# Convolution in bursts of two quads, and what its PSUM bank does between them: attention beside a long convolution on one core

## The chip, the core and the metric

One Trainium2 chip, one of its cores. A core has a matrix engine (TensorE, PE in the profile), a vector engine (VectorE, DVE), an engine for functions such as the exponential (ScalarE, ACT), GpSimd (POOL) and SyncE (SP); the last two issue most of the transfers here, which 16 DMA engines carry. Matrix products land in PSUM, eight banks of 128 partitions x 512 fp32 values; everything else lies in SBUF. The engines run side by side, each through its own list of instructions in order, and wait for each other by semaphores. The metric is the device time of one execution in microseconds (us).

## What is computed

Two independent blocks, joined along the last axis. A is attention: 2048 positions, 512 features, 32 heads of 16. B is a gated long convolution (H3): `kv` is a four-tap filter of `k` times `v`, convolved with a filter of 2048 taps per channel (`ssm_k`, with `ssm_D` added for the direct path), times `q`.

```python
def _A_ref(x, wqkv, wo):
    q, k, v = qkv[0], qkv[1], qkv[2]          # of x @ wqkv, per head
    scores = jnp.einsum("bhqd,bhkd->bhqk", q, k) * (Dh ** -0.5)
    p = _softmax(scores, axis=-1)
    o = jnp.einsum("bhqk,bhkd->bhqd", p, v)
    return o.transpose(0, 2, 1, 3).reshape(B, S, D) @ wo

def _B_ref(q, k, v, shift_k, ssm_k, ssm_D):
    ...
    kv = k_shift * v
    ...
    y = y + kv * ssm_D[None, None, :]         # y: kv convolved with ssm_k along S
    return q * y
```

The exponential of the scores is the large part of A: 32 heads x 2048 x 2048 = 134 million values.

## The kernel before

**A program written by a planner.** Python code (lines 540 to 1225) walks through the work chunk by chunk and appends instructions to one list per engine, in the order in which each engine will run them. Class `Eng` keeps a planned clock for each engine (`pe.t`, `dve.t`) and for each handle the planned time at which it will be done (`at(...)`); `dma` does the same for transfers, one after the other, at `DMA_KB` a microsecond and no sooner than `late` us after their issue. The planner decides by these times what comes next; on the chip the semaphores alone hold.

**Scores.** The work of A is 32 groups (four output column blocks `o` x four blocks of 512 queries x two), each of 64 blocks: a block is 128 keys x 512 queries of one head, and fills one PSUM bank. There are 2048 of them. `emit_qk(T)` takes the next chunk: `take_banks(T)` says which banks are free, even chunks from bank 0 up, odd ones from bank 5 down, up to `MOST` = 3 each. TensorE writes the scores (`qk_mm`, line 675, 32 rows a head, so that blocks of different heads run side by side), and ScalarE takes the exponential of the whole chunk in one instruction over its neighbouring banks (`emit_exp`, line 708), into the ring `PT` of 18 blocks. While ScalarE works on one chunk, TensorE fills the other banks.

**VectorE's blocks.** Some blocks go to VectorE instead (`dve_block`, `exp_on_dve`): line 750 reads the bank into `FX`, then three polynomial steps (line 757) and a last one (762) that leaves the block in `PTD`. The last block of a chunk of at least three is chosen, and its bank is `hold`-ed: ScalarE's chunk is then two blocks. `PV`, the product with the values (`emit_pv`, line 791), follows two chunks later into bank `PVB` = 6.

**Units.** Projections (`q`, `k`, `v`), the products that make `kv`, output products (`op`) and the transposes of finished convolution output (`turn`) are units of one bank each. Up to chunk `N_OPEN` = 68 they run in bank `BGB` = 7. Afterwards a *window* gives them a bank: when a unit falls due within `OPEN` = 80 chunks, `take_banks` holds one score bank for `LEN` = 3 chunks or more (`win`), and `unit_step` puts the units in, each as two halves, followed by an evacuation by VectorE. Chunks beside a window have a bank less. `jobs` lists the due chunks, from a planned total of `PLAN` = 710.

**Convolution.** From chunk 68 on, bank `BGB` belongs to the convolution. Channels go in quads of four, 128 quads. A quad needs its filters as shifted rows, `WR`: four loads of 512 KB by SP from the DRAM tensor `kz_scratch` (`load_wr`); `WR` has room for four quads, and the next load is issued when a quad's last product is done. A quad is 16 *lags*, each of four small products side by side (`conv_lags`, line 961). Four quads fill a bank; then VectorE copies it to `YB` (line 975, 512 columns). After eight quads a `turn` transposes `YB` (line 986), and line 995 multiplies by `q`. `emit_bg` says how many lags a chunk gets: at most `LAGS` = 6, no more than a running budget (`lags`, fed so that the convolution ends by `PLAN` - `END`, times `PACE`), and no more than fits before ScalarE would have to wait (`room`, with `MARGIN` = 0.35 us to spare). A quad starts when its load is planned to have landed `WAIT` = 1.5 us ago.

**Filler.** `warm_up` (line 1166) puts products with zero weights into TensorE's gaps, onto a bank in which a sum is open.

## Time and profile before

| | us |
|---|---|
| median of three runs | 841.38 (840.96 to 846.39) |
| span of the profiled execution | 840.8 |
| first exponential starts, last one ends | 9.67, 833.67 |
| TensorE clock granted, mean | 0.999 |
| filters read: 512 loads of 512 KB | 268 MB |
| data moved, mean over the span | 347 GB/s |

How to read the profile: its engine line gives busy time, share of the span and number of instructions. A group line reads "line engine operation out<-in shapes xcount | busy us, mean ns of one | idle time of the engine ahead of them, and who ended it". Busy time counts overlapping instructions once, while the mean is of each one's own duration. A line of waits reads "engine line <- releaser: us in total, times, longest". A line of windows gives start and end of a stretch, the busy time of each engine in it with the number of instructions, then the granted clock, the DMA share and GB/s.

Other groups that the text speaks of, from the same page:

```profile
L675 PE MATMUL PS<-QT,KTo 32*128 32x512 bf16 x2048 | 286.6, 384 | 34.6 <-ACT PT L708 6.6
L791 PE MATMUL PS<-PT,VA 128*32 128x512 bf16 x1820 | 196.8, 389 | 2.0 <-DVE DT L852 0.6
L1166 PE MATMUL PS<-IDN,ZW 128*32 128x512 bf16 (+4 forms) x632 | 162.4, 335 | 0.2
L757 DVE SCALAR_TENSOR_TENSOR EH<-EH,FX 128x512 f32<-128x512 f32 x456 | 305.1, 687 | 0.0
```

### The profile page before, as it was taken

To read this page: it belongs to the slowest core of one execution; us is meant where nothing else is said; L and a number is where in the kernel's file an instruction comes from. 1 tells how busy PE (TensorE), PEld (TensorE's weight loads), DVE (VectorE), ACT (ScalarE), POOL (GpSimd) and SP (SyncE) were. 2 spreads that over 40 slices of the span, in tenths; PEclk is the share of its full clock that TensorE was granted. 3 is DMA by queue.
4 is the path that set the end of the run, shared out by engine and by line. 5 is a ranking of instruction groups with operands and counts; after the bars stand their busy time and mean duration, and the time that the engine had idled before them with its cause. 6 is when DMAs were issued, how large, how long until landed. Compare 5 with 4: busy or idle time off the path is not lost.

```text
span 840.8 us, 30758 instructions
## 1 busy us (share of the span) xinstructions
PE 792.8 (94%) x13774; PEld 333.3 (40%) x13774; DVE 814.7 (97%) x1392; ACT 825.8 (98%) x726; POOL 77.6 (9%) x155
## 2 busy tenths in 40 slices
PE   8999999999999999999999999999999999999997
PEld 3343334444343434344434334443433333333442
DVE  3999999999999999999999999999999999999996
ACT  6999999999999999999999999999999999999997
POOL 3200220010100101000110010101002020000000
PEclk9999999999999999999999999999999999999999
DMA  9997199999999999999999999999999999999952
GB/s 230 216 310 285 50 371 370 354 347 408 392 408 394 393 402 338 371 326 378 330 379 408 384 340 359 377 405 398 406 408 379 351 394 409 409 316 391 405 200 76
DMA packets 109235, 291.42 MB, mean 347 GB/s; under 512 B 37680, under 2 KB 41648, under 8 KB 108720
## 3 DMA queue, kind: packets, MB, share of 16 engines
q1 hardware_dynamic: 102256, 280.80, 90.6%
q0 software_dynamic: 5648, 8.27, 3.2%
q8 instruction: 109, 1.79, 0.9%
q10 hardware_dynamic: 1200, 0.39, 0.2%
q14 instruction: 22, 0.18, 0.1%
HBM read 276.83 MB, written 6.42 MB: 337 GB/s over the span
## 4 chain that ended last, share of the span: by engine, by line
ACT 92%; PE 3%; DVE 3%; DMA 1%; issue 0%
ACT PT L708 92%; DVE EH L757 2%; PE PS L675 1%; PE PS L791 1%; DMA xT<-in_A_x_dram 1%; PE PS L961 1%; DVE PTD L762 1%; DVE FX L750 1%; PE PS L536 0%; PE PS L415 0%; PE PS L1166 0%; DVE DT L852 0%; ACT QT L920 0%; DVE DTN L863 0%; PE PS L902 0%
## 5 line engine op out<-in xcount | busy, mean ns | idle before, releaser
L708 ACT ACTIVATE PT<-PS 128x1536 bf16<-128x1536 f32 (+2 forms) x721 | 822.9, 1455 | 2.6 <-PE PS L675 2.6
L675 PE MATMUL PS<-QT,KTo 32*128 32x512 bf16 x2048 | 286.6, 384 | 34.6 <-ACT PT L708 6.6
L757 DVE SCALAR_TENSOR_TENSOR EH<-EH,FX 128x512 f32<-128x512 f32 x456 | 305.1, 687 | 0.0
L961 PE MATMUL PS<-WR,KV 128*15 128x128 bf16 (+15 forms) x8192 | 213.4, 219 | 1.1 <-issue 1.1
L791 PE MATMUL PS<-PT,VA 128*32 128x512 bf16 x1820 | 196.8, 389 | 2.0 <-DVE DT L852 0.6
L961 PEld LDWEIGHTS PS<-WR,KV 128*1 128x1 bf16 (+15 forms) x8192 | 144.7, 87 | 82.3 <-issue 47.1
L675 PEld LDWEIGHTS PS<-QT,KTo 32*128 32x128 bf16 x2048 | 72.7, 91 | 234.4 <-ACT PT L708 185.3
L1166 PE MATMUL PS<-IDN,ZW 128*32 128x512 bf16 (+4 forms) x632 | 162.4, 335 | 0.2
L750 DVE TENSOR_SCALAR FX<-PS 128x512 f32<-128x512 f32 x228 | 156.9, 690 | 2.4 <-PE PS L675 1.3
L762 DVE SCALAR_TENSOR_TENSOR PTD<-EH,FX 128x512 uint16<-128x512 f32 x228 | 155.7, 685 | 0.0
L757 DVE SCALAR_TENSOR_TENSOR EH<-FX 128x512 f32<-128x512 uint16 x228 | 155.7, 689 | 0.0
L259 POOL DMA_DIRECT2D QT<-QS x120 | 58.7, 497 | 481.5 <-DVE QS L442 165.7
L791 PEld LDWEIGHTS PS<-PT,VA 128*32 128x32 bf16 x1820 | 47.5, 93 | 108.6 <-issue 97.7
L791 PE MATMUL PS<-PTD,VA 128*32 128x512 bf16 x228 | 68.3, 383 | 0.3 <-DVE PTD L762 0.3
L1166 PEld LDWEIGHTS PS<-IDN,ZW 128*32 128x32 bf16 (+1 forms) x632 | 52.6, 96 | 23.8 <-issue 6.7
L852 DVE STREAM_TRANSPOSE DT<-PS 128x512 f32<-128x512 f32 x32 | 22.9, 716 | 6.2 <-PE PS L791 5.9
L975 DVE CAST YB<-PS 128x512 bf16<-128x512 f32 x32 | 22.0, 688 | 0.8 <-PE PS L961 0.8
L426 PE MATMUL PS<-WKV,xT 128*128 128x128 bf16 x256 | 18.8, 220 | 1.0 <-DVE KTo L451 0.7
L902 PE MATMUL PS<-WKV,OTN 128*128 128x512 bf16 x64 | 19.2, 384 | 0.3 <-DVE OTN L872 0.3
L403 PE MATMUL PS<-xT,WKV 128*128 128x512 bf16 (+1 forms) x64 | 18.1, 377 | 0.6 <-DVE KTo L451 0.5
L791 PEld LDWEIGHTS PS<-PTD,VA 128*32 128x32 bf16 x228 | 17.0, 95 | 2.0 <-DVE PTD L762 0.6
L394 PE MATMUL PS<-xT,WQ 128*128 128x512 bf16 x60 | 17.6, 384 | 0.2 <-DVE VA L473 0.2
(63 smaller groups left out, 211.8 us busy)
## 6 DMA issues: line engine op xcount, KB each, us to landing
WR<-kz_scratch SPq DMA_DIRECT2D x512, 512.0 KB, 8.0
kz_scratch<-WR SPq DMA_DIRECT2D x1, 2176.0 KB, 8.3
QN<-in_B_q_dram POOLq DMA_DIRECT2D x2, 1024.0 KB, 12.6
out_dram<-QN POOLq DMA_DIRECT2D x2, 1024.0 KB, 8.5
QT<-QS POOLq DMA_DIRECT2D x120, 16.0 KB, 5.2
out_dram<-OUTA POOLq DMA_DIRECT2D x12, 128.0 KB, 5.8
QN<-in_B_ssm_k_dram SPq DMA_DIRECT2D x1, 1024.0 KB, 8.5
OTN<-in_B_ssm_k_dram SPq DMA_DIRECT2D x1, 1024.0 KB, 9.1
```

Source lines behind the costliest of these rows:

```text
L259: f(outp, inp).then_inc(dsem.sem, 16)
L675: ins = e.matmul(PS[:, bank, :], lhsT=KTo[32 * s:32 * s + 32, OF[n_] % 2, kt * 128:(kt + 1) * 128], rhs=QT[32 * s:32 * s + 32, n_ // 2 % R ...
L708: h_exp[T] = act.op(lambda e: e.activation(PT[:, p0:p0 + n, :].rearrange("p b f -> p (b f)"), PS[:, banks[0]:banks[0] + n, :].rearrange("p ...
L750: h_f = urgent(lambda e: e.tensor_scalar(fx, PS[:, bank, :], FIX_ADD, FIX_HI, ALU.add, ALU.min), [h, h_last.get(i - R_FX)], slack=S_FX)
L757: st["h"] = dve.op(lambda e: e.scalar_tensor_tensor(eh, src, (A3, A2, A1)[j], frac, ALU.add, ALU.mult), [st["h"], h_last.get(i - R_EH)], u ...
L762: lambda e: e.scalar_tensor_tensor(out16, eh, A4, fx, ALU.mult, ALU.add),
L791: ins = e.matmul(dst, lhsT=w, rhs=rhs, start=(k == 0), stop=(k == KT - 1), tile_position=(0, 32 * s))
L852: h_t = urgent(lambda e: e.transpose(out=dt, in_=PS[:, PVB, :]), [h, h_mul.get(n - 1)], slack=S_T, us=(0.63, 0.751))
L902: ins = e.matmul(PS[:, bank, :], lhsT=OTN[:, PAIRS.index((o, qb)), t * 128:(t + 1) * 128], rhs=WO[:, o, :], start=(o == 0), stop=(o == 3))
L961: ins = e.matmul(PS[32 * c:32 * c + NB - n, BGB, 128 * (kk % 4):128 * (kk % 4) + 128], lhsT=KV[:, qd, n:NB, c], rhs=WR[:, r + c, 128 * (NB ...
L975: hh = urgent(lambda e: e.tensor_copy(YB[:, half, :].rearrange("p (k i) -> p k i", k=4), src), [h, h_yb[0]], slack=S_C, us=V512)
L1166: pe.op(lambda e, s=s, k=k, rhs=rhs, bank=bank, rows=rows, c0=c0, first=first: e.matmul(PS[32 * s:32 * s + rows, bank, c0:c0 + 128 * k], l ...
```

## The change

The convolution no longer runs a few lags in every chunk. It runs in bursts of two quads (`BURST` = `PER` = 2), and an owner is kept for its bank: `conv` during a burst, `w` while units use it, none otherwise. A burst begins when the filters of both quads are planned to have landed at least 1 us (`BWAIT`) ago and the bank is free; the budget `lags` and `PACE` are gone, and a chunk may take 12 lags. After two quads VectorE copies 256 columns to `YB`, and the bank is given up. Then units get a window in it if one is due within 40 (`OPEN_B`) and no burst is about to start. If no unit wants it, and no burst is near, VectorE's next block is put there, so that ScalarE's chunk keeps its three banks; or an odd chunk takes it as a fourth bank, next to banks 3 to 5. For that the convolution's bank becomes bank 6 and the PV bank 7. A window on a score bank is opened only if a unit is due at once while a burst holds the bank (`PRESS` = 0).

Due times are counted in thirds of the blocks that are done (`now`, `RATE_B`) rather than in chunks, `k` and `v` units are due earlier (`K_DUE` = 28), and the planner's picture of loads is changed: `DMA_KB` 382 for 396, and filter loads land no sooner than 6 us (`WR_LATE`) after their issue, 3.6 before.

```diff
-PVB = 6
-BGB = 7
+BGB = 6
+PVB = 7
-LAGS = 6
+LAGS = 12
...
-DMA_KB = 396
+DMA_KB = 382
+WR_LATE = 6.0
...
+    def spare_bank(T):
+        return T >= N_OPEN and owner[0] is None and len(queue) > LAST_BLKS + 12 and not conv_ready(T, SOON_D) and not near(T, OPEN_B)
+
+    def conv_ready(T, ahead):
+        st = state
+        if st["qd"] == C // 4 or st["qd"] % PER or st["lag"]:
+            return False
+        need = st["qd"] + BURST - 1
+        return need < wr_next[0] and kv_n[st["qd"] // 32] == 4 and at(h_wr[need]) + BWAIT <= pe.t + ahead
...
-        extra = dve_block(T, bl) if late["bank"] is None else None
-        d_bank = hold(T, banks, "d") if extra is not None else None
+        extra = d_bank = None
+        if late["bank"] is None:
+            if spare_bank(T) and at(bank_free[BGB]) + 0.13 <= max(pe.t, at(h_exp.get(T - 2)) + 0.13) + JOIN:
+                more = next_blocks(n + 1)
+                extra = dve_block(T, more)
+                if extra is not None:
+                    d_bank, bl, n = BGB, more, n + 1
+                elif T % 2 and not conv_ready(T, SOON_C):
+                    banks.append(BGB)
+                    bl, n = more, n + 1
+            if d_bank is None and BGB not in banks:
+                extra = dve_block(T, bl)
+                d_bank = hold(T, banks, "d") if extra is not None else None
...
-        return set(range(p, min(p + MOST, R_PT))) | (set(range(MOST)) if p + MOST > R_PT else set())
+        return set(range(p, min(p + MOST + 1, R_PT))) | (set(range(MOST + 1)) if p + MOST + 1 > R_PT else set())
...
-                h_wr[qd] = dma(sp, d_wr[i], WR[:, 4 * i + c, :], src, [h_kzw[0], dep])
+                h_wr[qd] = dma(sp, d_wr[i], WR[:, 4 * i + c, :], src, [h_kzw[0], dep], late=WR_LATE)
...
     def unit_step(T):
         if T < N_OPEN:
             stop = N_OPEN
-        elif "bank" in win:
+        else:
+            if "bank" not in win and owner[0] is None and near(T, OPEN_B) and not conv_ready(T, SOON_W) and len(queue) > LAST_BLKS:
+                owner[0] = "w"
+                win.clear()
+                win.update(bank=BGB, begin=T, stop=T + LEN_B)
+            if "bank" not in win:
+                return
             bank, stop = win["bank"], win["stop"]
...
-        st["lags"] = min(st["lags"] + min(PACE * st["left"] / left_us, RATE) * (pe.t - st["t"]), CAP)
-        st["t"] = pe.t
-        left = min(LAGS, int(st["lags"]), int((room(T) - pe.turn("C") - SWITCH) / LAG))
+        if owner[0] is None and conv_ready(T, 0.0) and at(bank_free[BGB]) <= pe.t + 0.1:
+            owner[0] = "conv"
+        if owner[0] != "conv":
+            return
+        left = min(LAGS, int((room(T) - pe.turn("C") - SWITCH) / LAG))
```

More of the change, by code (lines that the diff above doesn't have):

```diff
@@ L65 @@
 LEN = 3
+LEN_B = 5
+PRESS = 0
+OPEN_B = 40
+CLOSE_B = 50
+BWAIT = 1.0
+BURST = 2
+PER = 2
+SOON_C = 2.5
+SOON_D = 1.2
+SOON_W = 1.5
 WIN_D = 2
@@ L70 @@
 S_C = 0.3
-PLAN = 710
+RATE_B = 3.0
 JOIN = 0.05
@@ L75 @@
 Q_DUE = 24
+K_DUE = 28
 LOOK = 8
@@ L219, in bass_concat_heads__mha_block__ssm_conv_h3__prompt_kernel @@
     YB = sb("YB", [128, 2, 512])
+    YBF = YB[:, :, :].rearrange("p a n -> p (a n)")
     IDN = sb("IDN", [128, 128])
@@ L538, in first @@
         return h
-    h_qa = first(PS[:, 6, 0:256], WQ, 0, 256, [h_x[0][0], h_wq[0]], 0.11)
-    hk = first(PS[:, 7, 0:KEYS0], WK, 0, KEYS0, [h_x[0][0], h_wk[0]], 0.11 * KEYS0 / 256)
+    h_qa = first(PS[:, PVB, 0:256], WQ, 0, 256, [h_x[0][0], h_wq[0]], 0.11)
+    hk = first(PS[:, BGB, 0:KEYS0], WK, 0, KEYS0, [h_x[0][0], h_wk[0]], 0.11 * KEYS0 / 256)
     h_qb = first(PS[:, 5, 0:256], WQ, 256, 512, [h_x[0][1], h_wq[0]], 0.11)
@@ L543, in bass_concat_heads__mha_block__ssm_conv_h3__prompt_kernel @@
     for par in range(2):
-        for bank, c0, hp in ((6, 0, h_qa), (5, 256, h_qb)):
+        for bank, c0, hp in ((PVB, 0, h_qa), (5, 256, h_qb)):
             hh = bank_free[bank] = dve.op(
@@ L548, in bass_concat_heads__mha_block__ssm_conv_h3__prompt_kernel @@
         h_q[par] = hh
-    h_k0 = bank_free[7] = act.op(lambda e: e.activation(KTo[:, 0, 0:KEYS0], PS[:, 7, 0:KEYS0], ACT.Copy), [hk], us=(0.28, 0.42))
+    h_k0 = bank_free[BGB] = act.op(lambda e: e.activation(KTo[:, 0, 0:KEYS0], PS[:, BGB, 0:KEYS0], ACT.Copy), [hk], us=(0.28, 0.42))
     NBLK = NQB * NG * KT * 4
@@ L589, in take_banks @@
             banks = list(range(ends[1], 6))
-        if T >= N_OPEN and near(T, OPEN) and T >= win.get("last", 0) + REST and "bank" not in win and len(banks) > 2 and late["bank"] is None and len(queue) > LAST_BLKS + 18:
+        if T >= N_OPEN and near(T, PRESS) and "bank" not in win and owner[0] == "conv" and len(banks) > 2 and late["bank"] is None and len(queue) > LAST_BLKS + 18:
             b = hold(T, banks, "w")
@@ L594, in take_banks @@
         return banks
+    def spare_bank(T):
[6 more added lines that the diff above has]
+        return need < wr_next[0] and kv_n[st["qd"] // 32] == 4 and at(h_wr[need]) + BWAIT <= pe.t + ahead
     def near(T, most):
         job = next_unit(T)
-        return job is not None and job[0] - T <= most
+        return job is not None and job[0] - now(T) <= most
     def hold(T, banks, kind):
@@ L611, in bass_concat_heads__mha_block__ssm_conv_h3__prompt_kernel @@
     end = [10 ** 6]
+    owner = [None]
     h_held = {}
@@ L719, in pt_next @@
         p = pt_at[0]
-        return set(range(p, min(p + MOST, R_PT))) | (set(range(MOST)) if p + MOST > R_PT else set())
+        return set(range(p, min(p + MOST + 1, R_PT))) | (set(range(MOST + 1)) if p + MOST + 1 > R_PT else set())
     def dve_block(T, bl):
-        if len(bl) < 3 or WIN_D and "bank" in win and (part[0] or WIN_D > 1 and near(T, CLOSE)) or T < T_DVE or len(queue) < LAST_BLKS + 3 * (TAIL_GAP - N_LAST) + 3:
+        if len(bl) < 3 or WIN_D and win.get("bank", BGB) != BGB and (part[0] or WIN_D > 1 and near(T, CLOSE)) or T < T_DVE or len(queue) < LAST_BLKS + 3 * (TAIL_GAP - N_LAST) + 3:
             return None
@@ L953, in conv_lags @@
         r = 4 * wr_slot[qd]
-        if kk % 4 == 0 and n0 == 0:
+        if kk % PER == 0 and n0 == 0:
             deps.append(bank_free[BGB])
@@ L960, in fn @@
                 for c in range(4):
-                    ins = e.matmul(PS[32 * c:32 * c + NB - n, BGB, 128 * (kk % 4):128 * (kk % 4) + 128],
+                    ins = e.matmul(PS[32 * c:32 * c + NB - n, BGB, 128 * (kk % PER):128 * (kk % PER) + 128],
                                    lhsT=KV[:, qd, n:NB, c],
@@ L969, in conv_lags @@
             load_wr()
-            if kk % 4 == 3:
-                half = kk // 4
+            if kk % PER == PER - 1:
+                c0 = 128 * (kk + 1 - PER)
                 src = PS[:, BGB, :]
                 src = bass.AP(tensor=src.tensor, offset=PS[:, BGB, 127:128].offset,
-                              ap=[src.ap[0], [128, 4], [-1, 128]])
-                hh = urgent(lambda e: e.tensor_copy(YB[:, half, :].rearrange("p (k i) -> p k i", k=4), src),
-                            [h, h_yb[0]], slack=S_C, us=V512)
+                              ap=[src.ap[0], [128, PER], [-1, 128]])
+                hh = urgent(lambda e: e.tensor_copy(YBF[:, c0:c0 + 128 * PER].rearrange("p (k i) -> p k i", k=PER), src),
+                            [h, h_yb[0]], slack=S_C, us=(0.067 + 0.133 * PER, 0.193 + 0.133 * PER))
                 bank_free[BGB] = h_ybw[0] = hh
@@ L1009, in step, with now @@
     def step(n):
-        return PLAN * n // (NQB * NG)
+        return 4 * KT * n / RATE_B
+    def now(T):
+        return T if T < N_OPEN else (NBLK - len(queue)) / RATE_B
     jobs = [(step(2 * p) - Q_DUE, ("q", p)) for p in range(2, 16)]
-    jobs += [(step(OF.index(o)) - 16 + 4 * sc, (x, o, sc)) for o in (2, 3) for sc in range(4) for x in "kv"]
+    jobs += [(step(OF.index(o)) - K_DUE + 4 * sc, (x, o, sc)) for o in (2, 3) for sc in range(4) for x in "kv"]
     jobs += [(step(9 + 7 * c) - 8, ("kv", c + 2, i)) for c in range(2) for i in range(4)]
@@ L1016, in bass_concat_heads__mha_block__ssm_conv_h3__prompt_kernel @@
     jobs.sort(key=lambda j: j[0])
-    state = {"qd": 0, "lag": 0, "turn": False, "started": False, "lags": 0.0, "left": C // 4 * NB, "t": 0.0}
+    state = {"qd": 0, "lag": 0, "turn": False, "started": False}
     part = [None]
     def room(T):
-        lim = at(h_exp[min(T, end[0] - 1)]) - 0.47 - MARGIN
-        return lim - max(pe.t, at(bank_free[BGB]))
+        return at(h_exp[min(T, end[0] - 1)]) - 0.47 - MARGIN - pe.t
     def next_unit(T):
@@ L1027, in next_unit @@
         if state["turn"]:
-            return T, ("turn", state["qd"] // 8 - 1)
+            return now(T), ("turn", state["qd"] // 8 - 1)
         return next((j for j in jobs if ready(j[1])), None)
     def press(T):
-        load = max([(i + 1) * SLOT / max(due - T, 1) for i, (due, u) in enumerate(jobs)], default=0.0)
+        load = max([(i + 1) * SLOT / max(due - now(T), 1) for i, (due, u) in enumerate(jobs)], default=0.0)
         return SOON if load > FULL else NEAR if load > 0.75 * FULL else 0.0
@@ L1037, in unit_step @@
             stop = N_OPEN
-        elif "bank" in win:
+        else:
[5 more added lines that the diff above has]
+                return
             bank, stop = win["bank"], win["stop"]
-        else:
-            return
         tight = False
@@ L1054, in unit_step @@
             free = max(pe.t, at(bank_free[bank]) + 0.13)
-            late = T - due
+            late = now(T) - due
             if T < N_OPEN:
@@ L1060, in unit_step @@
             else:
-                ahead = (due - win["begin"] - 5) / SLOT
+                ahead = (due - now(T) - 5) / SLOT
                 over = TURN if u[0] == "turn" else 9.0 if ahead <= 1 else press(T)
@@ L1092, in emit_bg @@
         unit_step(T)
+        if owner[0] == "w" and part[0] is None and (T + 1 >= win["stop"] or not near(T, CLOSE_B) or conv_ready(T, 0.0)):
+            owner[0] = None
+            win.clear()
         if T == N_OPEN:
             assert not early
-            st["started"], st["t"] = True, pe.t
+            st["started"] = True
         if T - end[0] in tail_mm:
@@ L1101, in emit_bg @@
         if st["qd"] == C // 4 and not st["turn"]:
-            if T < end[0] + min(tail_mm) and h_wop[0] is not None:
+            if len(queue) <= LAST_BLKS and T < end[0] + min(tail_mm) and h_wop[0] is not None:
                 bank_free[BGB] = pe.op(keep_busy, [bank_free[BGB], h_wop[0]], run=MM, kind="F")
@@ L1112, in emit_bg @@
             return
-        left_us = max(1.14 * (PLAN - END - T), 1.0)
-        st["lags"] = min(st["lags"] + min(PACE * st["left"] / left_us, RATE) * (pe.t - st["t"]), CAP)
-        st["t"] = pe.t
-        left = min(LAGS, int(st["lags"]), int((room(T) - pe.turn("C") - SWITCH) / LAG))
+        if owner[0] is None and conv_ready(T, 0.0) and at(bank_free[BGB]) <= pe.t + 0.1:
[3 more added lines that the diff above has]
+        left = min(LAGS, int((room(T) - pe.turn("C") - SWITCH) / LAG))
         while left > 0 and st["qd"] < wr_next[0] and kv_n[st["qd"] // 32] == 4 and at(h_wr[st["qd"]]) + WAIT <= pe.t:
-            if st["turn"] and st["qd"] % 4 == 3 and st["lag"] + left >= NB:
+            if st["turn"] and st["qd"] % PER == PER - 1 and st["lag"] + left >= NB:
                 left = NB - 1 - st["lag"]
@@ L1122, in emit_bg @@
             n0 = st["lag"]
-            if n0 == 0 and st["qd"] % 4 == 0 and at(bank_free[BGB]) > pe.t - 0.2:
+            if n0 == 0 and st["qd"] % PER == 0 and at(bank_free[BGB]) > pe.t - 0.2:
                 break
@@ L1126, in emit_bg @@
             left -= n1 - n0
-            st["lags"] -= n1 - n0
-            st["left"] -= n1 - n0
             conv_lags(st["qd"], n0, n1)
@@ L1132, in emit_bg @@
                 st["qd"] += 1
-                if st["qd"] % 4 == 0:
+                if st["qd"] % PER == 0:
                     st["turn"] = st["turn"] or st["qd"] % 8 == 0
+                    owner[0] = None
                     break
@@ L1143, in filler_place @@
         if state["started"] and state["lag"]:
-            return BGB, 0, NB, 128 * (state["qd"] % 4), 1, False
-        if (not part[0] or state["started"]) and at(bank_free[BGB]) + 0.24 < limit and (state["qd"] % 4 == 0 or not state["started"]):
+            return BGB, 0, NB, 128 * (state["qd"] % PER), 1, False
+        if not part[0] and at(bank_free[BGB]) + 0.24 < limit and not state["started"]:
             return BGB, 0, 32, 0, 4, True
```

## The prediction

> **What bounds the kernel now.** I read the engine totals first, then ScalarE's groups with the shapes kept apart, then who waits for whom, then VectorE's groups, and last the loads, because the change paces itself by them.

> ```profile
> PE 792.8 (94%) x13774; PEld 333.3 (40%) x13774; DVE 814.7 (97%) x1392; ACT 825.8 (98%) x726; POOL 77.6 (9%) x155
> ```

> Three engines look full. TensorE is not: 162.4 us of its 792.8 is L1166, zero-weight filler put into gaps. ScalarE (ACT) and VectorE (DVE) are. The groups of ScalarE by shape, and its one row in the list of waits:

> ```profile
> L708 ACT ACTIVATE PT<-PS 128x1536 bf16<-128x1536 f32 x372 | 575.2, 1663 | 0.7 <-PE PS L675 0.7
> L708 ACT ACTIVATE PT<-PS 128x1024 bf16<-128x1024 f32 x346 | 395.4, 1229 | 0.4 <-PE PS L675 0.4
> L708 ACT ACTIVATE PT<-PS 128x2048 bf16<-128x2048 f32 x3 | 5.7, 1890 | 1.5 <-PE PS L675 1.5
> ...
> ACT PT L708 <- PE PS L675: 2.6, 5, 1.5
> ```

> The 721 exponentials are one unbroken row: the first starts at 9.67 us, the last ends at 833.67, and between them ScalarE waits 2.6 us in all. They overlap, so their own durations (1663 ns) are not what they cost. In the trace the end of one lies 917 ns behind the end before it if it takes two blocks, 1343 if three, 1771 if four: 427 ns a block and 64 ns an instruction. Check: 1820 x 0.4267 + 721 x 0.064 = 822.7 us, against 822.9 busy. So the time is 9.7 us of start + 64 ns x instructions + 427 ns x blocks + ScalarE's waits + some 7 us of tail. The profiled span, 840.8, is 0.6 under the median of the three runs, 841.38; I add changes to the median.

> Why 346 exponentials are short: the other blocks (2048 - 1820 = 228) are VectorE's, and each takes one of the chunk's three banks.

> ```profile
> L750 DVE TENSOR_SCALAR FX<-PS 128x512 f32<-128x512 f32 x228 | 156.9, 690 | 2.4 <-PE PS L675 1.3
> L975 DVE CAST YB<-PS 128x512 bf16<-128x512 f32 x32 | 22.0, 688 | 0.8 <-PE PS L961 0.8
> ```

> 228 of the 346 are these, seven are the closing chunks (N_TAIL), and the remaining 111 stand beside the windows, in which a projection unit holds a score bank (or a bank came late). Blocks over instructions give a handy form: instructions = (ScalarE's blocks + short chunks - four-block chunks) / 3 = (1820 + 346 - 3) / 3 = 721. **One bank given back, or one fourth bank, is worth 64 / 3 = 21 ns.** That is the size of everything this change can win.

> **Part by part.** *Windows to the convolution's bank.* The 111 short chunks lose their cause. A few stay, since a unit that is due during a burst still takes a score bank (PRESS): I take 100 away, 100 x 21.4 = 2.1 us; ends 0 and 111.

> *VectorE's blocks and fourth blocks in the free bank.* How long is it free? A burst is two quads, and needs two quads of filters, 4.19 MB. Views of the loads:

> ```profile
> WR<-kz_scratch SPq DMA_DIRECT2D x512, 512.0 KB, 8.0
> ...
> 440.00:460.00 20.00, 18.61 (x379) 8.30 (x376) 19.81 (x35) 20.00 (x18) 1.02 (x1) 1.00 1.03 408
> 460.00:480.00 20.00, 19.32 (x340) 8.18 (x341) 19.82 (x35) 20.00 (x19) 1.34 (x2) 1.00 1.02 387
> 480.00:500.00 20.00, 19.42 (x294) 7.17 (x286) 19.95 (x34) 20.00 (x20) 3.88 (x8) 1.00 0.99 353
> ...
> L961 PE MATMUL PS<-WR,KV x8192: 216/219/233, 93.6 to 820.3; 128*3 128x128 bf16 x16, 128*7 128x128 bf16 x15, 128*2 128x128 bf16 x14, 128*14 128x128 bf16 x14
> ```

> (The windows end in the granted clock, the DMA share and GB/s.) At 408 GB/s two quads take 10.3 us; over the convolution's whole stretch, 93.6 to 820.3 us, 128 quads took 5.68 each, 11.4 a pair. So a cycle is about 11 us, and the loads nearly fill the kernel before as after. Of the cycle the burst holds the bank for 32 lags: the shortest six-lag piece in the trace took 332 ns, 55 a lag, 1.8 us in all, but it is cut up by scores and PV (0.384 and 0.389 us each, mean rows of L675 and L791) in chunks of 0.92 to 1.34 us, so about five chunks, 5 to 6 us, and one more until the copy into YB has read it. 4 to 5 us stay free, 62 times, say 280 us. The units come first: 66 of them (14 q, 16 k and v, 8 kv, 12 output, 16 turns) at about 2.5 us (two pieces of 0.5, a 0.6 evacuation and its wait) are 165 us. In the 115 us left VectorE, which starts a block every 820 / 228 = 3.6 us, places about 30, and some 25 odd chunks get a fourth block: 55 x 21.4 = 1.2 us. Ends: nothing, and 200 (all 280 us used so): 4.3 us.

> [...]

> *The copy into YB.* 32 copies of 512 columns, 600 ns from start to start in the trace, become 64 of 256. The rows nearest are L451's, 690 ns at 512 columns and 424 at 256, so 0.6 - 0.27 = 0.33 us: 64 x 0.33 - 32 x 0.60 = 2 us more on VectorE, which has no gap to hide it (19.9 of every 20 us busy). A block costs it five steps of 0.6 = 3.0 us, so 0.7 blocks go to ScalarE: 0.3 us.

> *Feedback.* Each us that the end comes earlier takes 1/3 block from VectorE too, 0.14 us of ScalarE. So (2.1 + 1.2 - 0.3) / 1.14 = 2.6 us.

> *Hidden at nothing.* LAGS 12 and the dropped pace move the same 8192 convolution matmuls; PV sent off earlier because the ring must have four places free (MOST + 1) adds runs of 0.389 us. Both take the place of L1166's 162 us; fifty more PV runs are 20 us of that, and without that cover they would come out as waits of L708. Units due earlier (K_DUE 28) only fill the free bank. Exchanging PVB and BGB makes bank 6 the neighbour of 3 to 5, no more. SP issues the same 512 loads and POOL the same 120 QT copies.

> *The wait that could grow.* A burst stands on TensorE's queue ahead of the next scores. If its filters are late, scores wait, and ScalarE after the 0.35 us (MARGIN) that the planner leaves. Before, no row shows TensorE waiting for a load. I computed from the trace how long each quad's transfer took after the one before had landed: where the next was queued at least 5 us ahead (85 quads), 5.43 us in the mean, other traffic included; 8 of them over 6.4, worst where q of the second half is loaded and the first half's output written (460 to 485 us, up to 8.3). The planner will count 2048 / 382 = 5.36 us a quad, and apart from it some 17,000 KB of other transfers, 0.36 us a quad; and 6 us (WR_LATE) + 5.36 from an issue, where the trace shows 9.3 in quads that had no queue. Its picture is slower than the chip on average, and BWAIT gives 1 us on top. So I take no stall in the mean; ends 0 and 10 us.

> **The rivals.** *Late filters (20%).* Bursts take the loads as soon as the plan believes them landed, so the slack of 4 to 12 us between a quad's landing and its first matmul goes down to about 1. If the plan runs ahead of the chip, one quad in ten (the 8 in 85) is late by 1 to 2 us: 12 to 13 times 1.3 us is 16, of which the margin of 0.35 each takes 4, and the other gain 2.6: 841.4 + 12 - 2.6 = 851. It decides when the landing lies over 1.35 us behind the plan. Against it: the mean of 5.43 against 5.72 planned. A stronger form of it: if the loads came throughout as in the slower window above, 353 GB/s, the 268 MB of filters would need 760 us where there are some 715, and ScalarE would wait the other 45 us: 884. The windows of 407 and 408 GB/s speak against that; I give it 1 of the 20%. [...]

> *The bank is never free (12%).* Bursts stretched by short chunks, then units, fill all 11 us: units again take score banks and nothing goes into the sixth: gain 0 to 1, the YB copies 0.3: 841. In that case the change does not do what it says.

> *All of it is used (10%).* 311 banks, 6.6 - 0.3, over 1.14: 5.5 us, 836. A gain over 1% would need 8.4 us, that is 450 banks: there are only 346 short chunks, so fourth blocks would have to follow in a hundred.

> *Forecast (58%).* 841.4 - 2.6 = 838.8, its own range 837 to 840.5.

> **How the numbers follow.** 838.8 us. The range 835 to 850 takes in the full use below, and above it half of the late filters. A measurement of this kernel can tell about 1% from no change, 833 to 849.8. Faster 4% (the full use with more fourth blocks than I count), slower 16% (most of the late-filter case), same 80%.

> **What would show it.** Right: L708 about 670 times in place of 721, short ones near 215, four-block ones near 30, its wait for L675 below 5 us, L750 at 226 or 227, L975 64 times at some 0.42 us of its own, and the short chunks beside units gone. Wrong by late filters: TensorE's rows with waits on the load of WR, ScalarE's wait for L675 of 10 us and more. Wrong by occupancy: short chunks still over 300. Wrong in the price: fewer instructions, but ends not 64 ns apart from what blocks cost.

## The result, and the profile after

| | before | after |
|---|---|---|
| median, us | 841.52 (6 runs, 840.61 to 846.39) | 874.15 (6 runs, 870.65 to 875.98) |
| ratio | | 1.0376, 95% interval 1.0353 to 1.04 |
| span of the profiled execution | 840.8 | 874.2 |
| TensorE clock granted, mean | 0.999 | 0.974 |

The changed kernel is 3.8% slower, 33 us. I had forecast 838.8, with a range up to 850.

The engine totals after, the granted clock in 40 slices, and the queue that brings instructions:

```profile
PE 781.6 (89%) x13781; PEld 336.6 (38%) x13816; DVE 809.2 (93%) x1409; ACT 829.0 (95%) x670; POOL 78.0 (9%) x155
...
PEclk9999999999999999999988999998999899999999
...
q8 instruction: 109, 1.79, 0.8%
```

All three engines have lost share, so they wait for something together, and in four slices the clock is below 0.9. Before, the clock line was 9 throughout; the queue's line was there word for word but for its 0.9%, and I had not read it.

The groups of ScalarE by shape (they are line 743 now), with YB's copy and VectorE's blocks:

```profile
L743 ACT ACTIVATE PT<-PS 128x1536 bf16<-128x1536 f32 x440 | 635.3, 1566 | 22.0 <-PE PS L710 21.3
L743 ACT ACTIVATE PT<-PS 128x1024 bf16<-128x1024 f32 x197 | 223.1, 1137 | 11.0 <-PE PS L710 10.8
L743 ACT ACTIVATE PT<-PS 128x2048 bf16<-128x2048 f32 x27 | 52.5, 1943 | 1.5 <-PE PS L710 1.4
L785 DVE TENSOR_SCALAR FX<-PS 128x512 f32<-128x512 f32 x225 | 154.0, 684 | 17.2 <-PE PS L710 17.0
L1010 DVE CAST YB<-PS 128x256 bf16<-128x256 f32 x64 | 26.8, 419 | 18.9 <-PE PS L996 16.4 <-PE PS L1210 1.9
```

The counts are close to those that the prediction named: 665 exponentials (one more takes a single block), 197 short ones, 27 of four blocks. But a third column that was 0.7, 0.4 and 1.5 is now 22.0, 11.0 and 1.5. The list of waits says who makes them, and shows a releaser of TensorE that is no engine:

```profile
PEld PS L996 <- issue: 45.0, 102, 3.0
ACT PT L743 <- PE PS L710: 33.5, 39, 2.6
PEld PS L710 <- issue: 33.1, 82, 2.0
...
PE PS L996 <- issue: 22.0, 15, 2.8
```

"Issue" is time in which TensorE waits for nothing that the profile shows: no semaphore, no load. The convolution's products (L996) spend 22.0 us in 15 such waits, up to 2.8 us each. In the kernel before the same two kinds of rows read:

```profile
PEld PS L961 <- issue: 47.1, 193, 0.8
L961 PE MATMUL PS<-WR,KV 128*15 128x128 bf16 (+15 forms) x8192 | 213.4, 219 | 1.1 <-issue 1.1
```

So waits of the weight loads for "issue" are nothing new, and their sum is no sign. New are their length, 3.0 us at the longest in place of 0.8, and those of the products, 22.0 us in place of 1.1. One of them, in TensorE's timeline (start, length, instruction, in brackets the idle time before it):

```profile
436.11 0.40 PE L826 MATMUL PS<-PT,VA 128*32 128x512 bf16 x4
436.33 0.51 PE L996 MATMUL PS<-WR,KV 128*9 128x128 bf16 x23
439.63 0.59 PE L996 MATMUL PS<-WR,KV 128*4 128x128 bf16 x13 [2.80 <-issue]
440.15 0.61 PE L710 MATMUL PS<-QT,KTo 32*128 32x512 bf16 x3
```

TensorE stops inside a run of lags of the same quad, whose filters are there. When it goes on, a score product takes 0.61 us in place of 0.39. The stretches around it (busy time of each engine; at the end granted clock, DMA share, GB/s):

```profile
436.00:440.00 4.00, 1.20 (x43) 0.73 (x40) 1.31 (x3) 2.24 (x2) 0.00 (x0) 0.85 1.02 405
440.00:446.00 6.00, 6.00 (x39) 1.57 (x30) 4.67 (x8) 4.24 (x3) 0.00 (x0) 0.53 1.02 404
```

The same stretches of the kernel before:

```profile
436.00:440.00 4.00, 3.75 (x85) 1.68 (x84) 3.95 (x8) 4.00 (x5) 0.00 (x0) 1.00 1.02 408
440.00:446.00 6.00, 5.74 (x111) 2.36 (x112) 6.00 (x11) 6.00 (x6) 0.00 (x0) 1.00 1.03 408
```

For 6 us after the stall the clock is 0.53. ScalarE (the fourth of the engines) is busy for 2.24 of the first 4 us and 4.24 of the next 6; in the kernel before it was busy all the time, with nearly the same traffic.

**What TensorE waits for.** Its queue of instructions moves 109 packets of 16 KB. TensorE executes 13,816 weight loads and as many products, 27,632 instructions: 253.5 to a packet (253.6 and 253.9 in e2 and e4 below, with 79 and 173 packets). I counted the records from the start and marked number 188.9 and every 253.44th after it as a block border; no row gives these two numbers, they are set so that the stalls fit. Of 17 gaps of 1.4 us or more from one product's start to the next, 15 lie within 13 instructions of such a border, where chance would put two. A sign that needs no such count: the same 15 gaps end 1.25 to 1.61 us after a packet of the instruction queue has landed. A packet comes every 8 us, so chance would put one gap in some twenty there. The kernel before has no gap of 1.4 us.

At the border in the timeline above the block was used up 2.89 us after TensorE had entered it. The fetch of the next one had not begun: it began 3.44 us after that entry and landed 4.49 after it, and TensorE went on at 5.96. Over the blocks begun between 100 and 800 us, in us (marks are off by up to some ten instructions, so these figures by some tenths):

| | before | after |
|---|---|---|
| fetch starts after the border, median | 2.65 | 2.93 |
| fetch lands after the border, median | 3.71 | 3.97 |
| a block is used up in: shortest; 5% under; median | 5.01; 5.43; 6.85 | 2.89; 3.21; 7.27 |
| blocks used up in less than 5.4 (of 98 before, 92 after) | 5 | 26 |
| stalls of 1 us or more at a border | none | 13 |

So one block is in use and one more is on its way: in 106 of 108 blocks just one fetch begins. At the stalls mostly 5 to 6.3 us pass from the beginning of a block until TensorE can go on into the next (4.6 and 8.2 at the ends).

The kernel before used no block up in less than 5.01. Its worst borders are three stops of 0.44, 0.60 and 0.64 us, "issue" in the chain that ended last (at 192, 410 and 617 us), which end 1.45 to 1.59 us after a packet has landed. By these three the marks lie some 20 instructions late in that kernel; moved there, its fetch starts after 3.1 us and lands after 4.2, and its shortest block lasts 5.2. So the fetches were as late before; what is new is that blocks are used up sooner. A burst does that: two quads are 2 x 16 lags x 4 products, each with its weight load, 256 instructions, one block, in some 3 us.

**Where the 33.4 us went.** Span = first exponential's start + 64 ns an instruction + 427 ns a block + ScalarE's waits + tail, in the two profiled executions:

| us | before | after | difference |
|---|---|---|---|
| start of the first exponential | 9.67 | 7.74 | -1.9 |
| instructions and blocks (721 and 1820; 665 and 1823) | 822.7 | 820.4 | -2.3 |
| waits (what remains) | 1.2 | 38.9 | +37.7 |

The first row is not the change's doing: over the profiled executions of all kernels here it lies between 7.7 and 9.8, at 9.63 in e1 below, whose list of instructions is that of the changed kernel. Of the 38.9 us of waits, 33.5 stand in the profile's row; I put the rest down to overlap, since an exponential that waited does not lie beside the one before it (the mean of three-block ones fell from 1663 to 1566 ns, while the median step from end to end stayed at 1343). Some 15 of the 38.9 lie in stretches at half the clock. There are nine of these, of 3.41 or 6.83 us, 44.4 us in all, each in or soon after a gap of 1.74 to 3.01 us from one product's start to the next (1.5 to 2.8 us of it idle); of eleven such gaps nine were followed by one.

### The profile page after: what moved, and what is told of

Its sections match the earlier page's. It is cut to its first block, busy times and chain, and to the rows that moved or that the text cites. A ratio compares the mean times of both kernels' runs of the same rounds, so it can differ in the third digit from the quotient of the medians.

```text
span 874.2 us, 30729 instructions
## 1 busy us (share of the span) xinstructions
PE 781.6 (89%) x13781; PEld 336.6 (38%) x13816; DVE 809.2 (93%) x1409; ACT 829.0 (95%) x670; POOL 78.0 (9%) x155
## 3 DMA queue, kind: packets, MB, share of 16 engines
q1 hardware_dynamic: 102256, 280.80, 87.6%
## 4 chain that ended last, share of the span: by engine, by line
ACT 67%; PE 20%; DVE 7%; issue 4%; DMA 0%
ACT PT L743 67%; PE PS L710 6%; PE PS L996 5%; PE PS L826 4%; DVE EH L792 3%; PE PS L1210 2%; DVE FX L785 1%; DVE PTD L797 1%; PE PS L407 1%; DVE YB L1010 1%; DMA xT<-in_A_x_dram 0%; DVE DT L887 0%; PE PS L439 0%; PE PS L1021 0%; PE PS L937 0%
## 5 line engine op out<-in xcount | busy, mean ns | idle before, releaser
L743 ACT ACTIVATE PT<-PS 128x1536 bf16<-128x1536 f32 (+2 forms) x665 | 826.0, 1453 | 34.5 <-PE PS L710 33.5
L710 PE MATMUL PS<-QT,KTo 32*128 32x512 bf16 x2048 | 268.2, 391 | 35.7 <-ACT PT L743 15.4
L792 DVE SCALAR_TENSOR_TENSOR EH<-EH,FX 128x512 f32<-128x512 f32 x450 | 299.3, 680 | 0.0
L996 PE MATMUL PS<-WR,KV 128*16 128x128 bf16 (+15 forms) x8192 | 171.2, 220 | 22.2 <-issue 22.0
L1210 PE MATMUL PS<-IDN,ZW 128*32 128x512 bf16 (+3 forms) x674 | 167.2, 349 | 1.9 <-DVE DT L887 1.0
L996 PEld LDWEIGHTS PS<-WR,KV 128*16 128x16 bf16 (+15 forms) x8192 | 133.0, 87 | 63.1 <-issue 45.0
L710 PEld LDWEIGHTS PS<-QT,KTo 32*128 32x128 bf16 x2048 | 66.3, 91 | 220.8 <-ACT PT L743 151.4
L1210 PEld LDWEIGHTS PS<-IDN,ZW 128*32 128x32 bf16 x674 | 59.4, 98 | 68.5 <-issue 26.8
L1010 DVE CAST YB<-PS 128x256 bf16<-128x256 f32 x64 | 26.8, 419 | 18.9 <-PE PS L996 16.4
L272 POOL DMA_DIRECT2D out_dram<-OUTA x12 | 6.6, 553 | 130.8 <-DVE OUTA L945 119.4
L439 PEld LDWEIGHTS PS<-WKV,xT 128*128 128x128 bf16 x256 | 14.5, 98 | 9.6 <-issue 4.0
## 6 DMA issues: line engine op xcount, KB each, us to landing
WR<-kz_scratch SPq DMA_DIRECT2D x512, 512.0 KB, 8.4
```

The source lines that it names most:

```text
L272: f(outp, inp).then_inc(dsem.sem, 16)
L439: ins = e.matmul(PS[:, bank, 128 * j:128 * j + 128], lhsT=xT[:, dc, (4 * sc + j) * 128:(4 * sc + j + 1) * 128], rhs=WV[:, dc, o * 128:(o + ...
L710: ins = e.matmul(PS[:, bank, :], lhsT=KTo[32 * s:32 * s + 32, OF[n_] % 2, kt * 128:(kt + 1) * 128], rhs=QT[32 * s:32 * s + 32, n_ // 2 % R ...
L743: h_exp[T] = act.op(lambda e: e.activation(PT[:, p0:p0 + n, :].rearrange("p b f -> p (b f)"), PS[:, banks[0]:banks[0] + n, :].rearrange("p ...
L792: st["h"] = dve.op(lambda e: e.scalar_tensor_tensor(eh, src, (A3, A2, A1)[j], frac, ALU.add, ALU.mult), [st["h"], h_last.get(i - R_EH)], u ...
L996: ins = e.matmul(PS[32 * c:32 * c + NB - n, BGB, 128 * (kk % PER):128 * (kk % PER) + 128], lhsT=KV[:, qd, n:NB, c], rhs=WR[:, r + c, 128 * ...
```

## The experiments

The theory: TensorE's instructions come too slowly for a burst. Rivals were that dense small products themselves lower the clock, and the stalls follow (P in the expectations), and that the margin left for scores is too small for 12 lags, so that ScalarE waits whatever TensorE is fed (M). The filters themselves were out already: every quad had landed 4.4 us or more before its first product. Kernels compared with one another ran on one chip unless said.

**Half of the filter loads** (e1), the same plan, the same instructions, two rows of four loaded and used twice:

```diff
...
-            for c in range(4):
+            for c in range(2):
...
-                                   rhs=WR[:, r + c, 128 * (NB - 1 - n):128 * (NB - n)],
+                                   rhs=WR[:, r + c % 2, 128 * (NB - 1 - n):128 * (NB - n)],
```

> Changed part of the computation: of each quad's four filter rows only two are loaded, and the products of rows 2 and 3 use rows 0 and 1; the planner still counts four loads, so every compute engine has the same list of instructions in the same order as the changed kernel, and only the filter traffic is halved. Theory F (TensorE's instructions arrive too slowly in bursts: a block of some 254 instructions is used up in 3 to 4.5 us, while the next one is there only about 5.4 us after the block before it was begun): if the fetch is slow because it shares the DMA engines with the filters (F1), the stalls inside the bursts go and the time is 836 to 842 us with a clock of 1.00; if it is slow by itself (F2), stalls and clock stay and the time is 866 to 876. Rival P (dense bursts make the clock fall, and the stalls follow from that): same density, so 866 to 876 and clock 0.97 to 0.98. Rival M (the planner packs bursts with too little margin): same plan, so 866 to 876.

Measured: 839.71, ratio 0.9986 (0.9966 to 1.0007), clock 0.998. The data queue of the changed kernel, the same in e1 (packets, MB, share of 16 engines), and ScalarE's wait in e1:

```profile
q1 hardware_dynamic: 102256, 280.80, 87.6%
```

```profile
q1 hardware_dynamic: 65392, 146.56, 54.5%
```

```profile
ACT PT L743 <- PE PS L710: 5.1, 5, 1.7
```

The bursts are as dense as in the changed kernel (shortest block 2.83 us), but the fetch starts 0.84 us after the border (median) in place of 2.93, and three stalls of 1.2 to 1.5 us are left of thirteen. Bursts as dense did not lower the clock here (0.998, against 0.974 in the changed kernel), and the margin is the same: P and M fall. With half the filters beside it the fetch is 2.1 us earlier; by what path they hold it up, no run shows.

**Half of the convolution's instructions** (e2), one product of 256 columns for two lags, all filters loaded (half of the convolution's sums are then wrong):

```diff
...
-            for n in range(n0, n1):
+            for m in range(n0, n1, 2):
+                n = max(m, 1)
...
```

> Changed part of the computation: the convolution takes lags in twos, with one product of 256 columns in place of two of 128, so half of its sums are wrong; TensorE's column time, the loads, the plan and the bursts stay, the convolution's weight loads and products fall from 16,384 instructions to about half. Theory F: a burst has 128 instructions and not 256, a block of 254 lasts over 5.4 us almost everywhere, the stalls go: 836 to 842 us, clock 1.00. Rival P: the same columns stream in the same bursts, so the clock falls as before: 862 to 876, clock 0.97 to 0.98. Rival M: same packing, 862 to 876.

Measured: 837.34, 0.9943 (0.9918 to 0.9968), clock 0.999. Engine totals, ScalarE's two main groups and its wait:

```profile
PE 772.3 (92%) x10016; PEld 308.7 (37%) x10016; DVE 809.0 (97%) x1409; ACT 823.6 (99%) x670; POOL 77.7 (9%) x155
```

```profile
L743 ACT ACTIVATE PT<-PS 128x1536 bf16<-128x1536 f32 x440 | 657.6, 1707 | 0.1
L743 ACT ACTIVATE PT<-PS 128x1024 bf16<-128x1024 f32 x197 | 249.6, 1273 | 0.0
```

```profile
ACT PT L743 <- PE PS L710: 1.0, 1, 1.0
```

The exponentials are the same 440 and 197; their idle time is gone. The shortest block lasts over 7 us. All filters come in and the same columns pass through TensorE, so neither of these stalls it by itself. The stalls need both: the packets beside the filters, and a burst that uses them up.

**The other way round** (e4): the kernel before, each convolution product cut into two of 64 columns.

```diff
...
+                    for h0 in (0, 64):
...
-                                   rhs=WR[:, r + c, 128 * (NB - 1 - n):128 * (NB - n)],
+                                       rhs=WR[:, r + c, 128 * (NB - 1 - n) + h0:128 * (NB - 1 - n) + h0 + 64],
...
```

> The kernel before, with each convolution product of 128 columns split into two of 64, each with its own weight load: same result, same columns, twice the convolution's instructions (16,384 more), no bursts. Theory F: in the 727 us of the convolution about 42,400 instructions have to arrive, 167 blocks of 254; at 5.4 us each that is 902 us, so the time goes to about 1,000 us (950 to 1,050). Rivals P and M: nothing is burst here and TensorE has 162 us of filler to give for the extra instructions: 842 to 870 us.

Measured, in one run: 1110.46, more than expected, clock 0.897. Queue and waits:

```profile
q8 instruction: 173, 2.83, 1.0%
```

```profile
ACT PT L708 <- PE PS L675: 243.7, 201, 5.0
...
PEld PS L962 <- issue: 227.8, 334, 5.0
```

No burst is in this kernel. With 173 packets in place of 109 it stalls all through the convolution: 71 gaps of 1.4 us or more, each of them ending 1.2 to 1.6 us after a packet has landed. 47 stretches (228.7 us) are at half the clock, and ScalarE waits 243.7 us.

**Control and parts** (e9, e10): the kernel before with half the convolution's instructions, as in e2 (128 columns where the bank ends), and e2 with `spare_bank` returning False, so that only units use the bank.

> Control. Changed part of the computation: the kernel before with its lags taken in twos as in the run with half the instructions (products of 256 columns, 128 where the bank ends), so half of the convolution's sums are wrong; plan and loads as before. Theory F: the kernel before has no instruction stall over 1.2 us to lose, so nothing is won: 839.5 to 842 us, no difference from before. If fewer TensorE instructions were a gain by themselves, as far as the run with half of them showed it: 836 to 838.5.

> Changed part of the computation as in the run with half the convolution's instructions; besides, the convolution's bank between bursts serves units only, never a block of VectorE or a fourth block of ScalarE. This parts the two gains of the prediction. The plan has 686 exponentials over 1823 blocks, 821.8 us, against 665 and 820.4 with the spare bank used, and 721 and 822.7 before. By 64 ns an instruction: 1.4 us more than the run with the spare bank, 838.7 us (837.9 to 839.6), and about 2 us under before. If the extra bank gave its gain in another way than by the number of exponentials, it would be that of before, 840.5 to 842, or that with the bank, 837 to 837.6.

Measured: e9 839.73, 0.9975 (0.9967 to 0.9984); e10 838.9, 0.9969 (0.9959 to 0.998), with 686 exponentials. e9 is 2 us below the kernel before where I expected nothing: 1 us of ScalarE's few waits went, and its exponentials began at 7.95 in place of 9.67, which varies. Like for like, all with half the instructions: 839.73 without the change, 838.9 with the windows moved (-0.8), 837.34 with the spare bank too (-1.6; e2 ran on another chip). That is -2.4, and -0.32% by the ratios, where I had worked out -2.6. Free of the varying start, from the first exponential's start to the last one's end, the three profiled executions take 822.95, 821.80 and 820.86 us (64 ns an instruction and 427 ns a block give 822.7, 821.8 and 820.4): -1.15 and -0.94, 2.1 in all.

**Less dense, the simple ways.** Six lags a chunk with the planner's old picture of the loads (e3: `LAGS` 6, `DMA_KB` 396, `WR_LATE` 3.6), bursts of one quad (e7: `BURST` and `PER` 1), a budget of 4.8 lags a us with a cap of 8 (e8). In e7, e8 and all that follow `DMA_KB` and `WR_LATE` are set anew too (388 to 392, 4.2 to 5.0 us), since they pace the bursts.

> The changed kernel with at most 6 lags of a burst in one chunk in place of 12, and with the planner's picture of loads as it was before the change (396 KB a us, 3.6 us), without which the plan does not come to its end in time. Theory F: 6 lags and the rest of a chunk are some 66 TensorE instructions in 1.34 us, 254 in about 5.2 us, at the edge of what arrives; stalls become few and short, 838 to 848 us, clock above 0.995. Rivals P and M: half the density gives part of it back, 850 to 862. If filters come late after all, since the planner now believes in faster loads: waits on WR, 850 to 870.

> The changed kernel with bursts of one quad (BURST = PER = 1), loads planned at 388 KB a us and 5 us; copies into YB of 128 columns, 128 of them; up to 12 lags a chunk as in the changed kernel. Theory F: a burst is 128 instructions, a cycle of 5.5 us some 205, so a block lasts about 6.8 us and few stalls remain; the plan has 689 exponentials over 1826 blocks, 823.3 us against 822.7: 840 to 846 us, clock above 0.995. If density alone were the cause: 855 to 875.

> The changed kernel with a budget of 4.8 lags a us in bursts (at most 8 saved up), loads planned at 392 KB a us and 4.2 us. Theory F: 4.8 x 8 + 14 other instructions a us = 52, 254 in 4.9 us, a little under the 5.0 to 6.2 us a block takes to arrive: a few stalls of about 1 us; the plan has 689 exponentials over 1827 blocks, 823.7 us: 842 to 855 us.

Measured: e3 870.89, 1.0335 (1.0294 to 1.0377); e7 870.84, 1.0358 (1.0317 to 1.0398); e8 861.68, 1.0221 (1.0184 to 1.0259). All three miss, and lie above what was expected. Blocks are still used up in 4.0 us (e7) and 4.4 (e3, e8), because scores, PV and filler fill TensorE between the lags. And each has a second loss, one wait of 5.8 to 10.3 us. Waits of e3, and GpSimd's queue at that place (`QN<-in_B_q_dram` is the load of q's second half):

```profile
ACT PT L743 <- PE PS L710: 26.4, 28, 8.6
...
PE PS L710 <- DMA QT<-QS: 9.2, 1, 9.2
```

```profile
456.18 1.20 POOL L272 DMA_DIRECT2D out_dram<-QN  x1 [73.88 <-DVE QN L1030]
467.63 1.17 POOL L272 DMA_DIRECT2D QN<-in_B_q_dram  x1 [10.25 <-PE PS L710]
468.79 3.88 POOL L272 DMA_DIRECT2D QT<-QS  x8
```

The load waits until the output before it has left `QN`; eight copies into `QT` stand behind it on GpSimd, and the next scores need them. The profile names line 710 as what ended GpSimd's wait; but the load must wait for the output out of `QN`, issued up to 457.4, which is about 10 us earlier (in the kernel before the profile names that output, for a wait of 10.1 us). How the units fall decides whether copies get behind that load: in the changed kernel itself TensorE has no wait for copies into `QT`.

**A planner that counts blocks** (e5, e6): it counts TensorE's instructions, and lets a run of lags end ahead of a border that is reached less than 6.2 us (e5) or 5.6 us (e6) after the one before.

```diff
...
+        if pe.t < pe.edge_t + FETCH and pe.to_edge() < 8 * left + KEEP_I:
+            left = int(max(pe.to_edge() - KEEP_I, 0) / 8)
```

> The changed kernel, result unchanged, with a planner that counts TensorE's instructions: a burst may not take the lags that would use up a block of 253.4 instructions sooner than 6.2 us after the block was begun (the trace of the changed kernel shows 5.0 to 6.2 us from the start of a block to the resumption after a stall); loads planned at 388 KB a us and 5 us, so that the plan ends in time. Theory F: few stalls over 1 us, clock above 0.995; the plan has 674 exponentials over 1823 blocks, 821.0 us against 822.7 before, so 838 to 842 us. If density or margin were the cause, bursts are otherwise as dense as in the changed kernel (up to 12 lags a chunk): 860 to 875.

> As the run before with 5.6 us in place of 6.2. Theory F: some fetches are later than 5.6, so a few stalls of up to 0.6 us more, 838 to 846 us, clock above 0.99. Rivals: 860 to 875.

Measured: e5 868.7, 1.0301 (1.0254 to 1.0349); e6 863.07, 1.0258 (1.0224 to 1.0292). Missed again: the 16 instructions that it keeps back are used by the scores, PV and filler that follow, and these run into the border (shortest block in e5: 3.69 us). The whole of TensorE has to be held to the rate, not the convolution alone.

By their times alone e5, e6 and e7 lie in the ranges that had been given to density or margin. The traces decide against these: of the gaps of 1.4 us or more between two products' starts, 10 of 10 in e5, 10 of 10 in e6, 7 of 8 in e7, 5 of 7 in e3 and 4 of 5 in e8 end 1.2 to 1.65 us after an instruction packet has landed.

**The same, with the others' share kept back** (e11, e12): 13 instructions a us until the block may end are left for scores, PV and filler; the load of q's second half is issued 14 us later.

```diff
...
+        if pe.t < pe.edge_t + FETCH:
+            left = min(left, int((pe.to_edge() - KEEP_I - OTHERS * (pe.edge_t + FETCH - pe.t)) / 8))
...
-                load_qn(1, [ho])
+                later.append((pe.t + 14.0, ho))
```

> The changed kernel, result unchanged, with a planner that lets a burst use up a block of 253.4 TensorE instructions no sooner than 5.6 us after it was begun, and this time keeps instructions back for the scores, PV and filler that follow in the same time (13 a us); the load of the second half of q is issued 14 us later, so that it no longer holds up the copies into QT behind it on GpSimd's queue; loads planned at 390 KB a us and 4.5 us; units looked for 60 chunks ahead. The plan has 679 exponentials over 1821 blocks, 820.5 us, against 822.7 before. Theory F: stalls at block borders below 0.6 us, clock above 0.995, 838 to 844 us. If what is left in the runs with a limit is not the instruction blocks: 855 to 870.

> As the run before with 6.0 us a block, loads planned at 392 KB a us and 4.2 us, units looked for 70 chunks ahead. The plan has 692 exponentials over 1826 blocks, 823.4 us, above the 822.7 of before. Theory F: no stall over 1 us, clock above 0.998, 840.5 to 844 us, so the stalls are gone and nothing is won. Otherwise 855 to 870.

Measured: e11 852.57, 1.0134 (1.0118 to 1.0149); e12 851.14, 1.012 (1.0103 to 1.0137). In e12 no block is used up in less than about 5.4 us, and no border stalls 1 us. What is left has another cause; waits, and VectorE's timeline:

```profile
PE PS L857 <- DVE DT L918: 9.3, 7, 6.4
ACT PT L774 <- PE PS L741: 9.1, 7, 5.8
```

```profile
117.79 0.69 DVE L828 SCALAR_TENSOR_TENSOR PTD<-EH,FX 128x512 uint16<-128x512 f32 x1
121.02 0.69 DVE L486 TENSOR_SCALAR QS<-PS 128x512 bf16<-128x512 f32 x1 [2.54 <-DMA QT<-QS]
121.63 0.71 DVE L918 STREAM_TRANSPOSE DT<-PS 128x512 f32<-128x512 f32 x1
```

A q unit's evacuation into `QS` waits for the copies of the q unit before it; behind it on VectorE stands the transpose `DT`, and TensorE's PV waits for that, 6.4 us. The clock is halved for 13.7 us behind it.

**And with q units apart** (e13 with 5.8 us a block, e14 with 5.6): a q unit begins only when the copies of the one before are planned to have landed, 8 us after their issue.

```diff
...
-            return u[1] < R_Q or 2 * (u[1] - R_Q) + 1 in qk_done
+            return (u[1] < R_Q or 2 * (u[1] - R_Q) + 1 in qk_done) and (u[1] < 2 or 2 * u[1] - 1 in h_q and at(h_q[2 * u[1] - 1]) <= pe.t)
```

> As the run with 5.6 us a block, with 5.8 us, loads planned at 392 KB a us and 4.2 us, units looked for 60 chunks ahead, and a q unit begun only when the copies of the q unit before it are planned to have landed (planned 8 us after their issue). The plan has 681 exponentials over 1822 blocks, 821.0 us against 822.7 before. If instruction blocks and q copies are all of the loss: 838.5 to 842 us, clock above 0.998, faster than before by up to 3 us or the same. If bursts cost something more: 846 to 856.

> As the run before with 5.6 us a block and loads planned at 390 KB a us and 4.5 us; 682 exponentials over 1823 blocks, 821.5 us. If the two waits are all: 839 to 843 us, a little more stall than with 5.8; otherwise 846 to 856.

Measured: e13 844.88, 1.0021 (1.0004 to 1.0039); e14 844.17, 1.0032 (1.0011 to 1.0052). ScalarE's wait in e13:

```profile
ACT PT L774 <- PE PS L741: 7.0, 13, 1.1
```

Of the 33 us, 2 to 3 are left, with bursts and all convolution instructions in place. The rest are ScalarE's waits of up to 1.1 us, 7.0 us in all in e13 where the kernel before has 2.6, and they eat the 1.7 us that its plan wins. No version with the whole convolution was faster than the kernel before.

## Why the prediction was wrong

**The step that failed** is "*Hidden at nothing.* LAGS 12 and the dropped pace move the same 8192 convolution matmuls". They are the same matmuls, but a rate came with them. I priced a burst by its length on TensorE (55 ns a lag) and asked only whether other work still fits; I did not ask whether the instructions themselves arrive. The runs put 37.7 us of ScalarE's waits in the place of that nothing. The profile before had what was needed: 109 packets of 16 KB in the line of the instruction queue, 27,548 TensorE instructions, so 253 to a packet, in the trace a shortest block of about 5 us, and three short stops at "issue" in the chain that ended last. A burst's 256 instructions in some 3 us were outside all that the kernel had ever done.

**"The wait that could grow"** was looked for in the filters alone. They never were late: a quad had landed 4.4 us or more before its first product, 9.9 in the median, where the rival had this down to about 1. So the late-filter rival was wrong, and its 353 GB/s form too. That form stood nearest in time, 884, by a mechanism that did not act; that it came near is luck.

**The cover.** "Without that cover they would come out as waits of L708" was asked of fifty more PV runs. The cover was not used up: 674 fillers ran, 632 before. It did not cover these stalls: filler is products and weight loads on TensorE's list like all others, and ScalarE waited 33.5 us for L710, 2.6 us for L675 before.

**What was right.** The instruction price and the counts: 665 exponentials against 670, 197 short against 215, 27 of four blocks against 30, 64 copies of 419 ns against 420, and 225 VectorE blocks, one below the range given. Like for like the gain was 2.4 us against 2.6 (e9, e10, e2). The sum's size held for a kernel whose instructions arrive; the share given to everything on the slower side was too small, because the list of resources was not complete.

**The sign of its own test.** "TensorE's rows with waits on the load of WR" did not come. What came, products released by "issue" inside a run of lags, was on no list of mine.

## What to carry to other kernels

Before making a stage denser, count its instructions as well as its time: divide an engine's instructions by the packets of its instruction queue (253.5 here), and look in the trace how fast a block has been used up so far (5.01 us at the shortest before). Work that is moved closer together needs its instructions at that new rate, here 256 in some 3 us, beside whatever the DMA engines carry then (a data queue busy for 87.6% here). The sign in this case was a stall of a us or more "released by issue" inside a run of equal instructions (15 waits of L996, 22.0 us in all and up to 2.8 each, where the kernel before has 1.1 in all), above all where a packet of the instruction queue had landed 1.25 to 1.61 us before its end. Half the instructions (e2: 837.34 us, clock 0.999) and half the traffic (e1: 839.71 us, 0.998) told it from a clock that dense products bring down.

## What the runs showed of the hardware

**The clock.** In the changed kernel it fell to half nine times in or soon after a gap of 1.74 to 3.01 us from one product's start to the next, five times for 3.41 us and four times for 6.83; two of eleven such gaps were not followed by a fall. In e1, with bursts as dense, its mean was 0.998.
